# Fixing TensorE's order, turning k without it, and masking scores on two other engines in a gated-attention and SiLU kernel

## The chip, the cores and the metric

The kernel runs on one core of one Trainium2 chip. The metric is the time of one execution in device microseconds. Three runs of the kernel before took 563.61, 564.00 and 565.02 us, so the median is 564.0 us. The profiles come from one further execution each.

## The reference

Two blocks follow each other. The first is a recurrent gated attention over 4 batches, 8 heads, 768 tokens and 48 features for each head; the second is a feed-forward layer over the 3072 rows of its result.

```python
for t in range(S):                         # q, k, v, alpha: (4, 8, 768, 48)
    state = alpha[:, :, t, :, None] * state + einsum('bhd,bhe->bhde', k[:, :, t], v[:, :, t])
    y[:, :, t] = einsum('bhd,bhde->bhe', q[:, :, t], state)
x = y.transpose(0, 2, 1, 3).reshape(3072, 384)
h = x @ w_in                               # (384, 2048)
g = h * (1 / (1 + exp(-h)))
out = g @ w_out                            # (2048, 384)
```

The two weights arrive as 64-bit floats and are rounded to 32 bits on the chip.

## The kernel before

**Attention in chunks.** The sequence is cut into chunks of 128 tokens; with 4 batches that makes 24 chunks, numbered by `n`. A chunk is handled for all 8 heads at once, as 4 pairs of heads (`NP`). Each chunk passes through these stages:

- `products` (lines 674 to 715) brings alpha, k and q into a layout with features on partitions, scans alpha for its running product `u` (L699) and multiplies k by it (`kp`, L709, L713, L715). For the first 8 chunks (`n < NA`) TensorE turns the inputs (L694); later ones are loaded in quarters and turned by VectorE in blocks of 32x32 (L674).
- `quotient` divides: a second scan (L728) and a product with q (L733) give `qp`.
- `scores` multiplies kp by qp on TensorE (L757), cuts the result with the causal mask (`g`), turns kp into `kn` with tokens on partitions (TensorE L774, ScalarE copy L776) and scales the running state by the chunk's decay (L780). The mask is applied by ScalarE's copy and a GpSimd select (L763, L764) in chunks 0 to 3, and by VectorE's multiplication with a constant tile `mask` (L768) from chunk 4 on. From chunk 8 on only the halves of the scores that are needed are computed, so `blank` (L741) writes zeros into the PSUM banks beforehand.
- `values` forms y from g, v, the state and qp on TensorE (L800), and ScalarE copies it into `xt` (L805).
- `states` adds kn times v (L815) to the running state (VectorE L821).

The attention's PSUM tiles rotate through 3 banks (`ps_a`).

**Feed-forward pieces.** The dense work is cut into small pieces that are run between the attention stages. For the first two groups of 4 chunks the first layer is done plainly (`enter_plain`, L858, SiLU L861). From the third group on it is done with a fast matrix scheme that needs fewer products and more additions (`enter`: matmuls L882, ScalarE copies L888, VectorE additions L896, SiLU L893; `sums_x`, L562 to L567). The second layer is done in 7 products for each 2 chunks in the same manner (`leave`: matmuls L980, differences L985, copies L1010 and L1015, sums L1025 to L1036, stores L992 to L996). The chosen weights are rounded on the way in (`weights`: ScalarE L609, VectorE L623 to L625), and an audit reads the inputs once more and reduces them on VectorE (L653, L655, L663).

**The order of the work.** The program is written as 25 steps of 4 slots. In step `n`, slots are given to stages of chunk `n` (lag 0) and of chunk `n-1` (lag 1), and `fill` runs dense pieces after each slot until a running target is met (`marks`). A scheduler then reorders instructions on each engine, apart from the ones that `keep_in_program_order` holds in their stated order. All DMAs are issued by SP's queue: the loads of the next chunk's alpha, k and q (L465, 12 DMAs a chunk from chunk 8 on), of v (L482, L484), of the weights (L498), and the stores (L996).

The slots from chunk 8 on are:

```python
stages = [[(scores, 1)], [(products, 0)], [(values, 1), (states, 1)], [(quotient, 0), (blank, 0)]]
```

Of the kernel before, what the change touches and what calls it, by code (L numbers as in the profile page):

```python
# [355 lines left out]
def quotients(  # L356
# [20 lines left out]
    pe, dve, act, gps = nc.tensor, nc.vector, nc.scalar, nc.gpsimd  # L377
    B, H, S, D = q.shape
    C = 128
# [28 lines left out]
    rpool = pool("rpool")  # L408
    upool = pool("upool")
# [107 lines left out]
    def turns(x, n):  # L517

        return x[(n + 1) % 2 if n < NA else 0]
# [10 lines left out]
    mask = consts.tile([128, 2, C], F32, name="mask")  # L530
    gps.memset(mask, 1.0)
    for odd in range(2):
        for e in range(2):
            m = mask[CH * e : CH * e + CH, odd, :]
            gps.affine_select(m, m, pattern=[[1, C]], compare_op=ALU.is_ge, fill=0.0,
                              base=-CH * (e ^ odd), channel_multiplier=-1)
# [57 lines left out]
    def weights(which):  # L594

        pieces = [
            (w_in[:, t, c : c + 512], moe_w_in[t * 128 : t * 128 + 128, c : c + 512])  # L600
            for t, c in pieces_in
        ] if which == 0 else [
            (w_out[:, f, :], moe_w_out[f * 128 : f * 128 + 128, :]) for f in range(NFT)]
        def rounding(bits):
            n = bits.shape[1]
            up = upp.tile([128, 512], I32, name="up")[:, 0:n]

            tc.keep_in_program_order(
                act.activation(up, bits.bitcast(U32)[:, :, 0], AF.Copy, scale=2.0**-29))  # L609
            return up  # L610

        ahead = []
        for i, (dst, src) in enumerate(pieces):
            if not wide:
                act.dma_start(dst, src)
                yield
                continue
            assert which == 0 or conv_done[0] == n_conv[0]
            bits = coming.pop(0)
            up = ahead.pop() if ahead else rounding(bits)  # L620
            hi, w = bits[:, :, 1], dst.bitcast(I32)
            tc.keep_in_program_order(
                dve.tensor_scalar(w, hi, 3, 0x3FFFFFFF, ALU.logical_shift_left, ALU.bitwise_and))  # L623
            dve.scalar_tensor_tensor(w, hi, -(1 << 30), w, ALU.bitwise_and, ALU.bitwise_or)
            dve.tensor_tensor(w, w, up, ALU.add)  # L625
            if i + 1 < len(pieces):
                ahead.append(rounding(coming[0]))
            fetch()
            yield
# [46 lines left out]
    def products(n):  # L676
# [26 lines left out]
        kp = c["kp"] = turns(kps, n)  # L703
# [14 lines left out]
    def quotient(n, sg=None, q=None):  # L718
# [8 lines left out]
        p = turns(qps, n)  # L727
# [7 lines left out]
    def blank(n):  # L735

        if n < NA:
            return
        ps = ctxs[n]["blank"] = [ps_attn() for _ in range(2)]
        for t in ps:  # L740
            act.activation(t.rearrange("p j c -> p (j c)"), ident[:, 0:1].to_broadcast([128, 4 * C]),  # L741
                           AF.Copy, scale=0.0)

    def scores(n):
        c = ctxs[n]
        ci, b = c["ci"], c["b"]
        ps = c.pop("blank") if n >= NA else [ps_attn() for _ in range(2)]
# [11 lines left out]
        g = c["g"] = work.tile([128, 2, NP, C], F32, name="g")  # L759
        for u in range(2):  # L760
            if n < GB:

                act.copy(g[:, u], ps[u])  # L763
                gps.affine_select(g[:, u], g[:, u], pattern=[[0, NP], [1, C]], compare_op=ALU.is_ge,  # L764
                                  fill=0.0, base=0, channel_multiplier=-1)
                continue
            m = mask[:, :, None, :] if n >= NA else mask[:, 0:1, None, :]
            dve.tensor_tensor(g[:, u].rearrange("p (o j) c -> p o j c", o=2),  # L768
                              ps[u].rearrange("p (o j) c -> p o j c", o=2),
                              m.to_broadcast([128, 2, NP // 2, C]), ALU.mult)  # L770
        if ci < NCH - 1:
# [13 lines left out]
    def values(n):  # L785

        c = ctxs[n]
        ci, b, g, qp = c["ci"], c["b"], c["g"], c["qp"]
# [3 lines left out]
        todo = [(3 * j + i, vn[:, j, at : at + 32], g[:, u, j, :])  # L792
                for j in range(NP) for i, at, u in ((0, 0, 0), (1, 32, 0), (2, 80, 1))]
        todo += [(3 * j + 1, vn[:, j, 48:80], g[:, 1, j, :]) for j in range(NP)]
# [11 lines left out]
    def states(n):  # L806
        c = ctxs.pop(n)
        ci, b, vn = c["ci"], c["b"], c["v"]
        if ci < NCH - 1:

            ps = ps_attn()
            for j in range(NP):
                for i in range(4):
                    r = slice(32 * i, 32 * i + 32)
                    pe.matmul(ps[r, j, 0:D], lhsT=c["kn"][:, j, r], rhs=vn[:, 2 * j + i // 2, 0:D],  # L815
                              start=True, stop=True)
# [286 lines left out]
    marks = [2 * SLOTS + 2] + [(GB * i + 2 * GB) * SLOTS + 2 for i in range(len(phases))]  # L1103

    def settle():
# [4 lines left out]
        quads = pool("quads")  # L1110
        late["quads"] = {name: quads.tile([128, 32 + 4 * NP * D], F32, name=f"{name}t") for name in "akq"}
# [4 lines left out]
    def fill(step, slot):  # L1116

        at = step * SLOTS + slot
        if at < marks[0]:
            if step >= 1:  # L1120
# [12 lines left out]
    for step in range(STEPS):  # L1133
# [6 lines left out]
        elif step >= NA:  # L1140
            stages = [[(scores, 1)], [(products, 0)], [(values, 1), (states, 1)], [(quotient, 0), (blank, 0)]]
        for slot, group in enumerate(stages):
            for stage, lag in group:
# [8 lines left out]
                if stage is quotient and n + 1 < NT:  # L1152
                    load(n + 1)
                if stage is states and n + NV < NT:
                    load_v(n + NV)
            fill(step, slot)
# [23 lines left out]
    pe.matmul(ps, lhsT=good, rhs=mask[:, 0, C - 1 : C], start=True, stop=True)  # L1180
# [63 lines left out]
```

## Time and profile before

| | kernel before |
|---|---|
| median of 3 runs | 564.0 us |
| the profiled execution's own time | 563.47 us |
| its span, first to last instruction | 561.6 us |
| mean granted TensorE clock | 0.994 |
| TensorE (PE) busy | 543.9 us |
| VectorE (DVE) busy | 453.0 us |
| ScalarE (ACT) busy | 205.3 us |
| GpSimd (POOL) busy | 15.1 us |
| DMA | 63.81 MB, mean 114 GB/s |

A busy time counts an engine's instructions, with their ends modelled on TensorE, so a busy engine need not be working at its peak pace. In the profile every fp32 matmul other than a transpose shows as two records, so a product of 8 matmuls has 16. Lines such as L774 are lines of the kernel. In a timeline the columns are the start, the time that the row covers, engine, line, operation, operands and the count of records merged in the row; in brackets stands how long the engine was idle before it, and which engine released it.

### The profile page before, as it was taken

How to read it: one execution, taken by the hardware profiler on the slowest of the kernel's cores; microseconds unless marked ns; L12 is line 12 of the kernel's file. 1: busy time of each engine (PE TensorE's matmuls, PEld its weight loads, DVE VectorE, ACT ScalarE, POOL GpSimd, SP SyncE). 2: the span in 40 equal slices, each digit the busy share in tenths (PEclk: the TensorE clock that was granted, in tenths of full speed). 3: DMA queues.
4: the chain of work that ended last, by engine and by line, in shares of the span. 5: the costliest groups of instructions: out<-in, count | busy, mean ns of one | idle time of the engine just before them, and what ended most of it. 6: DMA issues, size and time to landing. Idle time of an engine off the chain costs nothing.

```text
span 561.6 us, 12420 instructions
## 1 busy us (share of the span) xinstructions
PE 543.9 (97%) x5074; PEld 492.6 (88%) x5074; DVE 453.0 (81%) x829; ACT 205.3 (37%) x406; POOL 15.1 (3%) x36
## 2 busy tenths in 40 slices
PE   5899999999999999999999999999999999999996
PEld 3688887998999999899989999999998999899995
DVE  5797899966999799986998897899895875857731
ACT  2566543213233342443433443434443342332100
POOL 4211000100000000000000000000000000000000
PEclk9899999999999999999999999999999999999998
DMA  9989971143443333333425544435522123334200
GB/s 206 230 241 223 234 183 34 43 126 100 100 107 89 73 97 87 101 87 85 131 70 160 142 108 134 130 81 153 136 69 81 53 85 118 99 94 125 71 30 26
DMA packets 94417, 63.81 MB, mean 114 GB/s; under 512 B 55312, under 2 KB 86032, under 8 KB 94352
## 3 DMA queue, kind: packets, MB, share of 16 engines
q1 hardware_dynamic: 94352, 62.94, 43.3%
q8 instruction: 41, 0.67, 0.5%
q14 instruction: 24, 0.20, 0.1%
HBM read 58.20 MB, written 4.72 MB: 112 GB/s over the span
## 4 chain that ended last, share of the span: by engine, by line
PE 75%; DVE 14%; DMA 5%; SPq 2%; issue 2%; ACT 1%; POOL 0%; DVEq 0%; ACTq 0%
PE ps_o L980 33%; PE ps_m L882 18%; PE ps_m L858 11%; PE ps_a L800 6%; DMA bits<-in_moe_w_out_dram 3%; PE ps_a L757 3%; DVE seen L663 2%; PE ps_a L774 1%; DVE g L896 1%; DMA bits<-in_moe_w_in_dram 1%; DVE u L699 1%; PE ps_a L815 1%; DVE w_out L625 1%; DVE p L728 1%; SPq L456 1%
## 5 line engine op out<-in xcount | busy, mean ns | idle before, releaser
L980 PE MATMUL ps_o<-w_out,g 128*128 128x192 f32 x768 | 133.6, 328 | 1.1 <-DVE o L994 1.1
L980 PEld LDWEIGHTS ps_o<-w_out,g 128*128 128x128 f32 x768 | 125.5, 190 | 3.9 <-DVE o L994 1.5
L980 PE MATMUL ps_o<-wt,g 128*128 128x192 f32 x576 | 100.0, 327 | 0.0
L980 PEld LDWEIGHTS ps_o<-wt,g 128*128 128x128 f32 x576 | 95.1, 190 | 1.5
L858 PE MATMUL ps_m<-xt,w_in 128*128 128x256 f32 x384 | 88.5, 382 | 1.0 <-ACT xt L805 1.0
L858 PEld LDWEIGHTS ps_m<-xt,w_in 128*128 128x128 f32 x384 | 71.0, 190 | 11.0 <-ACT xt L805 1.4
L882 PE MATMUL ps_m<-xc,w_in 128*128 128x256 f32 x288 | 70.1, 379 | 0.0
L882 PEld LDWEIGHTS ps_m<-xc,w_in 128*128 128x128 f32 x288 | 54.0, 190 | 6.4 <-DVE g L896 0.2
L663 DVE TENSOR_REDUCE seen<-bits 128x1 f32<-128x384 int32 (+2 forms) x65 | 42.4, 689 | 16.8 <-DMA bits<-in_moe_w_out_dram 16.5
L893 ACT ACTIVATE g<-g 128x1024 f32<-128x1024 f32 x32 | 33.1, 1055 | 57.5 <-DVE g L896 57.5
L985 DVE TENSOR_TENSOR g<-g 128x512 f32<-128x512 f32 x72 | 48.5, 686 | 5.6 <-PE ps_o L980 5.6
L882 PE MATMUL ps_m<-xc,wx 128*128 128x256 f32 x192 | 50.1, 383 | 0.0
L888 ACT COPY g<-ps_m 128x512 f32<-128x512 f32 x64 | 36.8, 587 | 36.1 <-PE ps_m L882 36.0
L780 ACT ACTIVATE st<-st,least 128x96 f32<-128x96 f32 x80 | 24.1, 364 | 58.4 <-DVE least L702 58.4
L882 PEld LDWEIGHTS ps_m<-xc,wx 128*128 128x128 f32 x192 | 35.0, 190 | 4.2 <-issue 0.4
L896 DVE TENSOR_TENSOR g<-ps_m,g 128x512 f32<-128x512 f32 x56 | 37.4, 683 | 0.8 <-PE ps_m L882 0.5
L699 DVE TENSOR_TENSOR_SCAN u<-al,one 128x516 f32<-128x516 f32 x24 | 29.1, 1212 | 10.4 <-ACT al L696 10.3
L728 DVE TENSOR_TENSOR_SCAN p<-al,inv 128x516 f32<-128x516 f32 x24 | 29.4, 1226 | 5.2 <-PE ps_a L800 4.9
L861 ACT ACTIVATE g<-ps_m 128x512 f32<-128x512 f32 x32 | 19.0, 595 | 39.2 <-PE ps_m L858 39.0
L800 PE MATMUL ps_a<-g,vn 128*32 128x128 f32 x768 | 28.0, 282 | 3.9 <-POOL g L764 3.9
L800 PEld LDWEIGHTS ps_a<-g,vn 128*32 128x32 f32 x768 | 20.3, 112 | 11.2 <-issue 5.5
L768 DVE TENSOR_TENSOR g<-ps_a,mask 128x512 f32<-128x512 f32 x40 | 25.7, 685 | 4.0 <-PE ps_a L757 3.7
(125 smaller groups left out, 620.7 us busy)
## 6 DMA issues: line engine op xcount, KB each, us to landing
bits<-in_moe_w_in_dram SPq DMA_DIRECT2D x24, 512.0 KB, 4.7
bits<-in_moe_w_out_dram SPq DMA_DIRECT2D x32, 384.0 KB, 3.4
at<-in_alpha_dram SPq DMA_DIRECT2D x64, 96.0 KB, 2.4
kt<-in_k_dram SPq DMA_DIRECT2D x64, 96.0 KB, 2.6
qt<-in_q_dram SPq DMA_DIRECT2D x64, 96.0 KB, 2.5
bits<-in_alpha_dram SPq DMA_DIRECT2D x9, 512.0 KB, 3.8
out_dram<-o SPq DMA_DIRECT2D x48, 96.0 KB, 1.9
an<-in_alpha_dram SPq DMA_DIRECT2D x8, 192.0 KB, 5.1
```

What stands on the lines that cost most here:

```text
L663: dve.tensor_reduce(seen[kind][which][:, i : i + 1], x, axis=AX, op=op, apply_absolute_value=True))
L699: dve.tensor_tensor_scan(u[:, end - 1 :: -1], sg[:, end:0:-1], one[:, end:0:-1], 0.0, ALU.mult, ALU.add)
L728: dve.tensor_tensor_scan(p[:, 0:end], sg[:, 0:end], iv[:, 0:end], 0.0, ALU.mult, ALU.add)
L768: dve.tensor_tensor(g[:, u].rearrange("p (o j) c -> p o j c", o=2), ps[u].rearrange("p (o j) c -> p o j c", o=2), m.to_broadcast([128, 2, ...
L800: pe.matmul(py[32 * at : 32 * at + 32, t, :], lhsT=w, rhs=x, start=(i < 4), stop=(i >= len(todo) - 4), skip_group_check=True)
L858: pe.matmul(ps[:, e, :], lhsT=w_in[:, t, (f + e) * 128 : (f + e + 1) * 128], rhs=xt[:, t, :], start=(t == 0), stop=(t == NKT - 1))
L882: pe.matmul(ps[:, e], lhsT=block_w(w)[:, 2 * pair + e], rhs=block_x(grp, x), start=(first and e == 0), stop=(e == 1), skip_group_check=True)
L888: act.copy(to, ps)
L893: act.activation(x, x, AF.Silu)
L896: dve.tensor_tensor(to, a, b, op)
L980: pe.matmul(ps, lhsT=x, rhs=w[:, i], start=(first and i == 0), stop=(i == HF - 1), skip_group_check=True)
L985: dve.tensor_tensor(cells(grp, h, pair, *to), cells(grp, h, pair, *x), cells(grp, h, pair, *y), ALU.subtract)
```

## The change

The change does five things.

- **TensorE in stated order.** `pe` becomes a small class whose `matmul` and `transpose` hold every instruction in its stated order. (In the changed program all TensorE instructions therefore carry the two lines of this class.)
- **Slots dealt anew.** From chunk 8 on: slot 0 `land` and `scores` of the chunk before, slot 1 `products`, slot 2 `quotient`, slot 3 `values` and `states` of the chunk before and `flip`. `p` gets a second buffer. The targets of `fill` move by one slot.
- **k turned by VectorE and by way of DRAM.** For chunks 8 to 19 `flip` turns kp in 32x32 blocks on VectorE, SP writes the result to a DRAM tile, and `land` reads it back with four DMAs in the order in which `states` needs it. Chunks 0 to 7 are turned by TensorE as before.
- **Masks by ScalarE and GpSimd.** VectorE's multiplication, the tile `mask` and `blank` go. Chunks 4 to 7 take the way of chunks 0 to 3. From chunk 8 on ScalarE copies only the halves that hold scores (two copies of 128x256 and four of 64x128), GpSimd selects in four pieces of 64x256, and the quarters that stay zero are cleared once.
- **Rounding moved.** The generator of the first weight stops once more: its ScalarE rounding is stated in slot 0 of step 1, its VectorE part a slot later.

```diff
-    pe, dve, act, gps = nc.tensor, nc.vector, nc.scalar, nc.gpsimd
+    dve, act, gps = nc.vector, nc.scalar, nc.gpsimd
+    class pe:
+        @staticmethod
+        def matmul(*args, **kw):
+            tc.keep_in_program_order(nc.tensor.matmul(*args, **kw))
+        @staticmethod
+        def transpose(*args):
+            tc.keep_in_program_order(nc.tensor.transpose(*args))
...
+    dram = pool("dram", 2, bass.MemoryType.DRAM)
...
+    decayed = fix.tile([128, 2 * NP * C], F32, name="g")
+    low, high = slice(0, CH), slice(CH, C)
+    earlier, later = [(low, 0), (high, 1)], [(low, 1), (high, 0)]
...
             up = ahead.pop() if ahead else rounding(bits)
+            if which == i == 0:
+                yield
...
-        p = turns(qps, n)
+        p = turns(qps if n < NA else [qps[0], late["p"]], n)
...
-    def blank(n):
...
+    def flip(n):
+        c = ctxs[n]
+        if n < NA or c["ci"] == NCH - 1:
+            return
+        t = late["turn"].tile([128, NP, C], F32, name="turn").rearrange("p c (j d) -> p c j d", j=NP)
+        dve.transpose(t, c["kp"].rearrange("p j (c i) -> p c j i", i=32))
+        c["flip"] = dram.tile([128, NP * C], F32, name="flips")
+        nc.sync.dma_start(c["flip"], t.rearrange("p c j d -> p (c j d)"))
+
+    def land(n):
+        c = ctxs[n]
+        if "flip" in c:
+            c["kn"] = work.tile([128, NP, C], F32, name="kn")
+            x = c.pop("flip").rearrange("(r d) (i x) -> i d r x", r=4, i=4)
+            for i in range(4):
+                nc.sync.dma_start(c["kn"][32 * i : 32 * i + 32], x[i])
...
-            m = mask[:, :, None, :] if n >= NA else mask[:, 0:1, None, :]
-            dve.tensor_tensor(g[:, u].rearrange("p (o j) c -> p o j c", o=2),
-                              ps[u].rearrange("p (o j) c -> p o j c", o=2),
-                              m.to_broadcast([128, 2, NP // 2, C]), ALU.mult)
-        if ci < NCH - 1:
+        for u in range(2 if n < NA else 0):
+            act.copy(g[:, u], ps[u])
+            gps.affine_select(g[:, u], g[:, u], pattern=[[0, NP], [1, C]], compare_op=ALU.is_ge,
+                              fill=0.0, base=0, channel_multiplier=-1)
+        if n >= NA:
+            ps = [x.rearrange("p (o j) c -> p o j c", o=2) for x in ps]
+            for u in range(2):
+                act.copy(swapped[:, :, u, :, CH:], ps[u][:, :, :, CH:])
+            for r, o in earlier:
+                for u in range(2):
+                    act.copy(swapped[r, o, u, :, 0:CH], ps[u][r, o, :, 0:CH])
+            for at, half in ((CH, later), (0, earlier)):
+                for r, o in half:
+                    x = swapped[r, o].rearrange("p u j c -> p (u j) c")[:, :, at : at + CH]
+                    gps.affine_select(x, x, pattern=[[0, NP], [1, CH]],
+                                      compare_op=ALU.is_ge, fill=0.0, base=0, channel_multiplier=-1)
+        if n < NA and ci < NCH - 1:
             ps_k = ps_attn()
             for j in range(NP):
                 pe.transpose(ps_k[:, j, :], c["kp"][:, j, :], ident)
...
-    marks = [2 * SLOTS + 2] + [(GB * i + 2 * GB) * SLOTS + 2 for i in range(len(phases))]
+    marks = [2 * SLOTS + 2] + [(GB * i + 2 * GB) * SLOTS + 3 for i in range(len(phases))]
...
-            if step >= 1:
+            if at == SLOTS:
+                next(conv[0])
+            elif step >= 1:
                 convert(0, (at - SLOTS) * 3 // (marks[0] - SLOTS) + 1)
...
-            stages = [[(scores, 1)], [(products, 0)], [(values, 1), (states, 1)], [(quotient, 0), (blank, 0)]]
+            stages = [[(land, 1), (scores, 1)], [(products, 0)], [(quotient, 0)],
+                      [(values, 1), (states, 1), (flip, 0)]]
...
+            if step * SLOTS + slot == (NA + 1) * SLOTS - 1:
+                x = decayed.rearrange("p (o i c) -> p o i c", o=2, c=C)
+                for r, o in later:
+                    gps.memset(x[r, o, :, 0:CH], 0.0)
```

## The prediction

> **What bounds the kernel now.** I read the page first (busy shares, then the chain of work that ended last), then the timeline of TensorE from 0 to 562 us, then the groups by form, the waits, and the order of instructions on each engine in both programs.
>
> ```profile
> PE 543.9 (97%) x5074; PEld 492.6 (88%) x5074; DVE 453.0 (81%) x829; ACT 205.3 (37%) x406; POOL 15.1 (3%) x36
> ...
> PE 75%; DVE 14%; DMA 5%; SPq 2%; issue 2%; ACT 1%; POOL 0%; DVEq 0%; ACTq 0%
> ```
>
> TensorE is busy for 97% of the span and makes up 75% of the chain. Because matmul ends are modelled, I checked the starts. In the timeline, 16 records of L980 take 2.60 us and 12 records of L882 or L858 take 2.59 us wherever they follow each other. From 25 us on, nearly every start comes at that pace. The stretch 25.18 to 128.69 us (103.5) is filled by its records at these paces (97 us) and some thirty switches of shape at 0.1 to 0.2 us. So from 25 us on, **a microsecond of TensorE work is a microsecond of the span**, and VectorE's 81% matters only where it makes TensorE wait. After 25 us the waits are few:
>
> ```profile
> 232.24 1.13 PE L882 MATMUL ps_m<-xt,w_in 128*128 128x256 f32 x4 [0.40 <-DVE g L896]
> ...
> 294.85 1.13 PE L882 MATMUL ps_m<-xt,w_in 128*128 128x256 f32 x4 [0.34 <-ACT g L888]
> ...
> 483.69 2.87 PE L980 MATMUL ps_o<-w_out,g 128*128 128x192 f32 x16 [1.07 <-DVE o L994]
> ```
>
> Measured by starts these three cost 0.7, 0.5 and 1.2 us, about 2.5 us with the smallest ones.
>
> **What the Trainium skill says.** "TensorE: Matmul & The Clock Gate", Part 4, puts a transpose at about 275 ns in a kernel. The trace's records agree (L774 median 273 ns), but they overlap: four take 0.4 to 0.5 us. "VectorE: DVE Perf Modes", The three transpose paths, says that VectorE transposes only inside 32x32 blocks; so the change needs DRAM to move the blocks. L674 shows its price, 1.11 us for 128x512. "DMA: Bandwidth & Descriptors", Anatomy of one DMA, gives about 2.0 us fixed for one transfer; the page agrees (1.9 us for an output store, 2.6 for a k load). "SBUF — State Buffer", Who interferes with whom, says a VectorE instruction with two SBUF inputs contends with a GpSimd one that reads SBUF. The trace has a sign of it: the two selects L764 took 1.94 us at 14.94 us beside VectorE's weight rounding and 1.23 us at 21.17 us with VectorE idle.
>
> **The change part by part.**
>
> *k turned without TensorE.* Of 20 chunks that turn k at L774, 12 (chunks 8 to 19) stop. The same program shows a step with and without it:
>
> ```profile
> 243.29 0.90 PE L757 MATMUL ps_a<-p,kp 48*64 48x128 f32 x32
> 244.12 0.66 PE L774 MATMUL ps_a<-ident,kp 128*128 128x128 f32 x4
> 244.62 1.03 PE L882 MATMUL ps_m<-xc,wx 128*128 128x256 f32 x4
> 245.48 1.03 PE L882 MATMUL ps_m<-xc,w_in 128*128 128x256 f32 x4
> ...
> 413.62 0.90 PE L757 MATMUL ps_a<-p,kp 48*64 48x128 f32 x32
> 414.45 1.13 PE L882 MATMUL ps_m<-xc,wx 128*128 128x256 f32 x4
> 415.42 1.03 PE L882 MATMUL ps_m<-xc,w_in 128*128 128x256 f32 x4
> ```
>
> From the scores to the second L882 row it is 2.19 us with the turn (243.29 to 245.48) and 1.80 without (413.62 to 415.42). So 12 x 0.40 = **4.8 us** leave the bound, nearly certain (4.5 to 5.2).
>
> What it adds lies elsewhere. VectorE: 12 transposes at 1.11 = 13.3 us. SP: 12 x 5 issues at about 0.44 (its k loads) = 26 us over some 250; 6.3 MB, and the DMA engines are at 0.3 to 0.45 of capacity there. The trip is one store (2 us), then four loads (4 x 0.44 + 2.6): some 6.5 us. It starts late in step n, its loads stand in slot 0 of step n+1, and `states` reads in slot 3. A step takes 21 us, so over 10 us are left. What waits behind it on SP: in the new order half of the next chunk's alpha loads and all its k and q loads stand behind the store, and behind v's loads, which wait for `states`. From `states` on, SP needs 3 v and 1 or 2 alpha issues and a landing, about 4.5 us; VectorE has 4.7 to 4.8 us of other work before it transposes alpha. This is tight: 0 to 1 us of VectorE wait a step, and scores stand more than a slot later. I take 0 on TensorE. `turn` has one buffer, so the next k also waits for the store; some 10 us of VectorE work lie between.
>
> *Masks.* VectorE loses 40 multiplications (25.7 us busy) and, late, its wait for scores. ScalarE loses 32 blanks (L741, 0.60) and 12 copies of k (0.58), gains 2 copies 128x256 and 4 of 64x128 a late chunk. By its copies of 512, 384 and 192 columns (587, 475, 315 ns) these are 0.37 and 0.26, so 1.78 a step: just what leaves (2 x 0.60 + 0.58). Chunks 4 to 7 add 8 x 0.59. GpSimd gains 8 selects at 0.87 and 64 half-size ones (estimate 0.3 to 0.55 each, from L764's 0.63 to 1.08 for twice the columns): 19 to 35 us on an engine that does nothing there. If each half-size one holds VectorE up by 0 to 0.2 us (weight rounding beside L764 ran 0.2 to 0.4 long), that is 0 to 13 us of VectorE. Its balance is -25.7 + 13.3 + (0 to 13): 12 us less to nothing. Mask latency is scores to select, about 4 us, and y now stands five pieces (13 us) behind the scores. Cost on the path: nothing while that cover stands.
>
> *Slots and order.* The quotient moves from slot 3 to 2, y and states from 2 to 3, p gets two buffers. So qp is ready a slot before its scores, and VectorE's wait for y (L728, 4.9 us) goes. The price: scores now follow y by a single piece, 2.6 us, on three PSUM buffers, and the second scores bank is y's. It is free once ScalarE has copied y (L805), which in every second step stands behind four SiLUs (L893) that wait for VectorE. Today's example: y ends at 363.7, the SiLUs at 364.8, so the copy could end at 365.3, 1.6 us after y; the scores would want it 3.1 us after. 1.5 us of room. I take +1.0 us in all, between 0 and 16 (1 us in every late step). For the old waits that vanish I take -1.0 (0 to -2.5).
>
> *Rounding.* At the start the static order on ScalarE puts one weight rounding before the first scores' copies where there were two, and the second waits for its DMA:
>
> ```profile
> 11.39 0.69 ACT L609 ACTIVATE up<-bits 128x512 int32<-128x512 uint32 x1 [1.92 <-DMA bits<-in_moe_w_in_dram]
> ...
> 13.73 0.67 ACT L609 ACTIVATE up<-bits 128x512 int32<-128x512 uint32 x1 [1.65 <-DMA bits<-in_moe_w_in_dram]
> ...
> 14.30 1.05 ACT L763 COPY g<-ps_a 128x512 f32<-128x512 f32 x2
> ...
> 14.94 1.94 POOL L764 TENSOR_SCALAR_AFFINE_SELECT g<-g 128x512 f32<-128x512 f32 x2 [7.91 <-ACT g L763]
> ...
> 15.89 0.64 PE L800 MATMUL ps_a<-g,vn 128*32 128x128 f32 x4 [3.62 <-POOL g L764]
> ```
>
> The copies can start near 12.1, 2.2 us sooner. Not all gets through: the third L858 piece met its weights just in time (32.23 to 32.54 us), and VectorE's w_out chain ends at 101.5 us where TensorE waits 0.23; that chain loses one mask pair, 1.3 us. I take -1.3 (0 to -2.2).
>
> *Sum.* -4.8 - 1.3 - 1.0 + 1.0 = -6.1 us. The profiled run took 563.5 us (span 561.6 and 1.9 around it), 0.5 under the median of three, 564.0. So 557.4 by the profiled run, 557.9 by the median; I say **557.5 us**.
>
> **Rivals.** (1) *The bound holds and the sum comes through*, 553 to 562 us, 0.64. For it: the saturated timeline, and a part that is counted, not inferred. (2) *Only the turn is saved and small new waits eat it*: VectorE is busy 33 to 39 of each 40 us between 200 and 440, so a late load, a select on the shared port or a late L896 each hold TensorE a little; no gain at the start, +4 us: 563 us, 0.13. (3) *Slower: the bank of y.* If SiLUs and so the y copy come later than the 1.5 us of room, TensorE stops at the scores with all its dense work behind it. From a mean of 0.44 us on each of 16 late steps it uses up the gain of 7.1 us that stands without it, from 0.6 the kernel is measurably slower; at 1 us a step it gives 557.5 - 1 + 16 = 572 us. For it: ScalarE waits 57.5 us for L896 before L893, up to 6.7 at a time. Against it: most of that is ScalarE early, not TensorE late. 0.23. That k still comes from TensorE in part can be excluded: the new order has no such transposes after chunk 7.
>
> **How the numbers follow.** 0.3% (1.7 us) is about what a measurement of this kernel can tell from no change: 562.3 and 565.7 are the edges. Case 1 is faster throughout; of case 2, 0.03 is faster and 0.10 the same; case 3 is slower. So 0.67, 0.10, 0.23. The range, 553 to 568, leaves some 0.04 below (all waits gone and the start's full gain) and 0.15 above (rival 3 from 0.7 us a step). Case 1's own range is 553 to 562.
>
> **What would show it.** Right: no L774 rows after chunk 7; L757 followed within 0.85 us by a dense row; first L800 near 13.7 us; late steps some 0.4 us shorter; no TensorE wait above 0.5 us at scores or at `states`. Wrong: TensorE waits before L757 released by ScalarE's y copy (rival 3), before `states` by the loads of k (trip too slow), or VectorE above 92% in the late stretches with TensorE waiting for L896 (rival 2).

## The result, and the profile after

The changed kernel takes 580.05 us (median of 4 runs, 578.9 to 581.0), the kernel before in the same rounds 563.81. The ratio is 1.0286, with a 95% interval of 1.0258 to 1.0315: **slower by 16.1 us** (0.0286 x 563.81). The forecast was 557.5 us, range 553 to 568. The profiled execution has a span of 579.2 us.

This is the page of the changed kernel: the busy shares, the slices of TensorE and of its granted clock, and the chain that ended last. Every TensorE instruction now has line L384 (matmul) or L388 (transpose), so it is read by its tiles. The *trip* below is the new way of k: VectorE's flip (L757), its store to DRAM (L759), the four loads back (L767).

```profile
PE 544.3 (94%) x5026; PEld 491.0 (85%) x5026; DVE 446.1 (77%) x801; ACT 207.7 (36%) x466; POOL 50.1 (9%) x106
...
PE   5899998999998999999999799599999999999996
...
PEclk9999999999999999999999799989999999999999
...
PE 57%; DVE 18%; DMA 14%; SPq 5%; issue 2%; ACT 2%; POOL 0%; DVEq 0%; ACTq 0%
```

TensorE has 48 instructions less, as foreseen, yet the same busy time. Its share of the chain fell from 75% to 57%; DMA rose from 5% to 14% and SP's queue from 2% to 5%. VectorE is *less* busy than before. There are two holes in TensorE's row, each with a lower clock in the same slice or the next. The timeline of TensorE shows them:

```profile
321.40 0.52 PE L384 MATMUL ps_a<-vn,kn 128*32 128x48 f32 x32
326.11 5.23 PE L384 MATMUL ps_o<-w_out,g 128*128 128x192 f32 x16 [4.18 <-DVE o L1028]
331.27 0.90 PE L384 MATMUL ps_a<-p,kp 48*64 48x128 f32 x32
332.10 1.13 PE L384 MATMUL ps_m<-xc,w_in 128*128 128x256 f32 x4
...
369.95 0.52 PE L384 MATMUL ps_a<-vn,kn 128*32 128x48 f32 x32
376.60 5.49 PE L384 MATMUL ps_o<-w_out,g 128*128 128x192 f32 x16 [6.12 <-DVE o L1028]
```

After the state products, TensorE waits for VectorE to empty the bank of an output (L1028), 4.2 and 6.1 us long. In both cases an audit of 1.2 to 1.3 us (L677) stands right ahead of that instruction in VectorE's order. The product that follows takes 5.23 and 5.49 us where 16 matmuls of this kind take 2.76 to 2.87 elsewhere. The windows view (busy time of each engine, then granted clock) has the reason:

```profile
core 0: us, PE busy (x) PEld busy (x) DVE busy (x) ACT busy (x) POOL busy (x), PEclk, DMA share, GB/s
...
326.00:331.30 5.30, 5.19 (x20) 4.97 (x20) 1.97 (x5) 0.00 (x0) 0.00 (x0) 0.53 0.80 207
...
376.60:382.00 5.40, 5.40 (x16) 4.97 (x16) 3.50 (x9) 0.00 (x0) 0.00 (x0) 0.50 0.90 229
```

The clock is at half after each stop. So the two stops cost 4.2 + 2.5 and 6.1 + 2.7, together 15.5 us, nearly the whole difference. The rest roughly cancels. The start gained what was foreseen (first y product at 13.85 us instead of 15.89; first dense piece at 23.44 instead of 25.18), and undisturbed late steps are 21.4 and 20.5 us from y to y instead of 21.8 and 20.9. Smaller waits eat that gain.

**Why VectorE was late.** These are VectorE's waits for DMAs from 128 to 455 us, after (in all, times, longest), together 20.2 us, and then the only row of before in that window for a turn of alpha, k or q or for the audit:

```profile
DVE al L688 <- DMA at<-in_alpha_dram: 11.1, 6, 4.6
...
DVE al L688 <- DMA kt<-in_k_dram: 3.9, 3, 2.9
DVE seen L677 <- DMA bits<-in_alpha_dram: 2.6, 1, 2.6
DVE seen L677 <- DMA bits<-in_moe_w_in_dram: 2.6, 2, 2.4
```

```profile
DVE al L674 <- DMA at<-in_alpha_dram: 0.5, 1, 0.5
```

Now SP's queue in one step of the changed kernel, with its neighbour VectorE (start, duration). First SP, from one store of the flipped k to the next:

```profile
299.94 0.32 SPq L759 DMA_DIRECT2D flips<-turn  x1
300.31 0.92 SPq L478 DMA_DIRECT2D at<-in_alpha_dram  x2
301.64 0.35 SPq L667 DMA_DIRECT2D bits<-in_alpha_dram  x1
302.08 0.96 SPq L495 DMA_DIRECT2D vn<-in_v_dram  x1
303.14 1.27 SPq L497 DMA_DIRECT2D vn<-in_v_dram  x2
304.45 1.07 SPq L478 DMA_DIRECT2D at<-in_alpha_dram  x2
305.57 1.85 SPq L478 DMA_DIRECT2D kt<-in_k_dram  x4
307.46 1.85 SPq L478 DMA_DIRECT2D qt<-in_q_dram  x4
309.36 2.93 SPq L767 DMA_DIRECT2D kn<-flips  x4
...
322.30 0.33 SPq L759 DMA_DIRECT2D flips<-turn  x1
```

Then VectorE in the same step:

```profile
306.40 1.22 DVE L677 TENSOR_REDUCE seen<-bits 128x1 f32<-128x1024 f32 x1 [2.65 <-DMA bits<-in_alpha_dram]
308.13 1.11 DVE L688 STREAM_TRANSPOSE al<-at 128x512 f32<-128x512 f32 x1 [0.51 <-DMA kt<-in_k_dram]
...
321.56 0.71 DVE L757 STREAM_TRANSPOSE turn<-kp 128x512 f32<-128x512 f32 x1
...
324.58 1.21 DVE L677 TENSOR_REDUCE seen<-bits 128x1 f32<-128x1024 f32 x1
325.71 0.35 DVE L1028 TENSOR_TENSOR o<-ps_o,u 128x192 f32<-128x192 f32 x1
```

The rows show a **loop of two in-order queues**. The store waits on SP for VectorE's flip, the last thing VectorE does for a chunk; SP issued nothing from 294.93 to 299.94 us. Over the window such waits are 35.6 us (SP's waits at the output's stores are longer, 75.4 us, but before they were 63.5):

```profile
SPq L759 <- DVE turn L757: 35.6, 8, 6.8
```

The Trainium skill says why it is SP that stands ("DMA: Bandwidth & Descriptors", Anatomy of one DMA): the DMA engines don't wait on semaphores, the issuing queue does, ahead of the issue. The trace agrees: the idle 5.0 us are SP's. The next chunk's alpha, k and q, the audit and v stand behind the store in SP's order. VectorE turns alpha when it has landed, and 13.4 us after that comes to the next flip. Store to store is 22.36 us here, while TensorE's own step is 20.5 (21.4 every second time). With every engine in order, VectorE is late for whatever it meets next, and in the two stops that is L1028. That the store alone closes this loop is not shown: one of the experiments (e7_loads_pool) opens it with the store still in SP's queue.

How far ahead the loads run can be counted: from the end of the last issue of alpha (L465, L478) to VectorE's turn of it (L674, L688), over chunks 8 to 23. Before, the median is 13.2 us, and over 12 in the last nine chunks. After, the median is 2.6 us; in 12 of 16 chunks it is between 1.9 and 3.1, about the time that an alpha load takes to land (2.4 us). The lead was gone in those chunks. A long lead isn't needed, though: the fastest kernel below (c2_masks_old_slots) has a median of 4.2.

### The profile page after: what moved, and what is told of

Same layout as the page of the kernel before. It is cut to its first block, busy times and chain, and to the rows that moved or that the text cites. A ratio compares the mean times of both kernels' runs of the same rounds, so it can differ in the third digit from the quotient of the medians.

```text
span 579.2 us, 12563 instructions
## 1 busy us (share of the span) xinstructions
PE 544.3 (94%) x5026; PEld 491.0 (85%) x5026; DVE 446.1 (77%) x801; ACT 207.7 (36%) x466; POOL 50.1 (9%) x106
## 4 chain that ended last, share of the span: by engine, by line
PE 57%; DVE 18%; DMA 14%; SPq 5%; issue 2%; ACT 2%; POOL 0%; DVEq 0%; ACTq 0%
PE ps_o L384 25%; PE ps_m L384 23%; PE ps_a L384 8%; DMA bits<-in_moe_w_out_dram 7%; DVE seen L677 3%; DVE g L930 3%; SPq L478 3%; DVE turn L688 2%; DMA bits<-in_moe_w_in_dram 2%; PE ps_a L388 1%; DMA kn<-flips 1%; DMA qn<-in_q_dram 1%; DVE u L713 1%; SPq L767 1%; DVE g L1019 1%
## 5 line engine op out<-in xcount | busy, mean ns | idle before, releaser
L384 PE MATMUL ps_o<-w_out,g 128*128 128x192 f32 x768 | 139.6, 337 | 13.0 <-DVE o L1028 11.6
L384 PEld LDWEIGHTS ps_o<-w_out,g 128*128 128x128 f32 x768 | 130.1, 196 | 17.2 <-DVE o L1028 13.1
L384 PE MATMUL ps_m<-xt,w_in 128*128 128x256 f32 x480 | 113.7, 383 | 3.1 <-ACT xt L838 2.8
L384 PEld LDWEIGHTS ps_m<-xt,w_in 128*128 128x128 f32 x480 | 89.0, 190 | 16.6 <-ACT xt L838 3.8
L384 PE MATMUL ps_o<-wt,g 128*128 128x192 f32 x576 | 99.7, 326 | 0.0
L384 PEld LDWEIGHTS ps_o<-wt,g 128*128 128x128 f32 x576 | 95.1, 190 | 1.6 <-issue 0.2
L384 PE MATMUL ps_m<-xc,w_in 128*128 128x256 f32 x288 | 70.7, 382 | 0.4 <-ACT part L922 0.4
L677 DVE TENSOR_REDUCE seen<-bits 128x1 f32<-128x384 int32 (+2 forms) x65 | 42.5, 689 | 25.4 <-DMA bits<-in_moe_w_out_dram 18.8
L384 PEld LDWEIGHTS ps_m<-xc,w_in 128*128 128x128 f32 x288 | 53.7, 190 | 7.4 <-ACT part L922 0.7
L802 POOL TENSOR_SCALAR_AFFINE_SELECT g<-g 64x256 f32<-64x256 f32 x64 | 29.8, 466 | 291.2 <-ACT g L795 288.1
L384 PE MATMUL ps_m<-xc,wx 128*128 128x256 f32 x192 | 50.0, 383 | 1.0 <-ACT g L922 1.0
L922 ACT COPY g<-ps_m 128x512 f32<-128x512 f32 x64 | 36.6, 586 | 35.8 <-PE ps_m L384 35.6
L930 DVE TENSOR_TENSOR g<-ps_m,g 128x512 f32<-128x512 f32 x56 | 37.2, 682 | 4.8 <-PE ps_m L384 4.5
L384 PEld LDWEIGHTS ps_m<-xc,wx 128*128 128x128 f32 x192 | 35.2, 190 | 5.2 <-ACT g L922 1.3
L688 DVE STREAM_TRANSPOSE al<-at 128x512 f32<-128x512 f32 x16 | 17.8, 1115 | 16.6 <-DMA at<-in_alpha_dram 12.6
L922 ACT COPY part<-ps_m 128x512 f32<-128x512 f32 x32 | 18.7, 585 | 26.9 <-PE ps_m L384 21.3
```

The costliest lines, as they stand in the source:

```text
L384: tc.keep_in_program_order(nc.tensor.matmul(*args, **kw))
L677: dve.tensor_reduce(seen[kind][which][:, i : i + 1], x, axis=AX, op=op, apply_absolute_value=True))
L688: dve.transpose(to.rearrange("p g (b j) -> p g j b", j=4), x[:, :, :, 0:32])
L802: gps.affine_select(x, x, pattern=[[0, NP], [1, CH]], compare_op=ALU.is_ge, fill=0.0, base=0, channel_multiplier=-1)
L922: act.copy(to, ps)
L930: dve.tensor_tensor(to, a, b, op)
```

## The experiments

Two theories stood at first. Q: the trip's DMAs in SP's queue starve VectorE. O: the stated order and the new slots make the stops by themselves. A third, M, put it on the masks. In the expectations, "checks" are the kernel's audit (L677).

### One part taken away or done alone

**k back on TensorE** (e1_k_on_pe), so no flip, store or loads:

```diff
-        if n < NA or c["ci"] == NCH - 1:
-            return
+        return
...
-        if n < NA and ci < NCH - 1:
+        if ci < NCH - 1:
             ps_k = ps_attn()
```

> The changed kernel, but k is turned by TensorE again in all chunks (four transposes and ScalarE's copy), so VectorE's turn of k, its store to DRAM and its four loads are gone; order, slots, masks and rounding stay as changed. Theory Q (the trip's DMAs stand in SP's queue ahead of the next chunk's loads, VectorE starves, falls behind and stops TensorE at the first product of an output): the two stops of 4.2 and 6.1 us at L384 (ps_o) are gone with their slow products, some 15.6 us, a few of the small stops as well, and 4.8 us of turns come back: about 567 us, 562 to 570. Theory O (the stated order and the new slots make the stops by themselves): the stops stay, 580 + 4.8 = 585, 582 to 588. Theory M (the masks on ScalarE and GpSimd delay VectorE): also 582 to 588.

Measured: 569.5 us, ratio to before 1.0093 (1.0066 to 1.0121), 10.5 us below the changed kernel though 4.8 us of turns (the forecast's figure) are back. Both long stops are gone. Theory Q holds for these; 5.3 us above before stay.

**The trip on GpSimd's queue** (e2_trip_pool):

```diff
-        nc.sync.dma_start(c["flip"], t.rearrange("p c j d -> p (c j d)"))
+        gps.dma_start(c["flip"], t.rearrange("p c j d -> p (c j d)"))
...
-                nc.sync.dma_start(c["kn"][32 * i : 32 * i + 32], x[i])
+                gps.dma_start(c["kn"][32 * i : 32 * i + 32], x[i])
```

> The changed kernel, but the trip's store and its four loads of k are issued from GpSimd's queue instead of SP's; VectorE still turns k and the same bytes move. Theory Q: SP is free for the next loads, VectorE's waits for alpha, k and the audited data go from 12.6 us to about before's 1, the two long stops go: 564 us, 556 to 568. Theory O or M: nothing of it matters, 578 to 583. If it is the volume of the trip on the DMA engines and not its place in the queue, the waits stay too: 578 to 583. A new wait may come: the masks (L802) stand behind the loads in GpSimd's queue, then y waits for them.

Measured: 568.3 us, ratio 1.0061 (1.0041 to 1.0081). The bytes are the same, so the volume was not the cause: 11.8 us hung on the queue, and on the order in which SP's other DMAs then stand. The time is just above theory Q's range. VectorE's waits for alpha, k, q and the audit did not go to 1 us but from 20.2 to 10.5, and in e1_k_on_pe to 7.8: what counts is not their sum but what stands behind each.

**TensorE's order left free** (e4_pe_free):

```diff
-            tc.keep_in_program_order(nc.tensor.matmul(*args, **kw))
+            nc.tensor.matmul(*args, **kw)
```

(and likewise for the transposes)

> The changed kernel, but TensorE's order is left to the scheduler instead of stated. Theory O: it can go around the late eviction bank, the two stops of 4.2 and 6.1 us go: 564 us, 560 to 568. Theory Q: VectorE is late whatever TensorE does, stops of this size stay at the first product of an output or move: 576 to 584; the scheduler puts the state products next to the following scores, so loads of k may show up less.

Measured: 572.9 us, 1.0147 (1.0121 to 1.0173). It lies between the two. The longest wait at L1028 in the profile is 1.3 us, so the free order goes around the late bank, but it moves the state products and steps become uneven (27 and 15 us). So the two long stops needed a late VectorE *and* a TensorE that may not do other work.

**The kernel before with the order stated** (b1_order_only):

```diff
-    pe, dve, act, gps = nc.tensor, nc.vector, nc.scalar, nc.gpsimd
+    dve, act, gps = nc.vector, nc.scalar, nc.gpsimd
+
+    class pe:
+        @staticmethod
+        def matmul(*args, **kw):
+            tc.keep_in_program_order(nc.tensor.matmul(*args, **kw))
+
+        @staticmethod
+        def transpose(*args):
+            tc.keep_in_program_order(nc.tensor.transpose(*args))
```

> The kernel before, with TensorE's order stated and nothing else changed. Theory O with the stated order as its cause: 570 us or more. Theory Q or M: no change, 563.8 plus or minus 1.7.

Measured: 566.8 us, 1.0042 (1.0026 to 1.0057). The stated order costs 2.4 us, more than the 1.7 that theories Q and M allowed for, less than the 6 of O. In its profile y is 2.0 us later than before at 110.68 us and 2.4 at 447.60. TensorE waits for a w_in piece (1.57 us at 50 us) and for ScalarE's y copies: 0.60, 0.60 and 1.47 us at 24, 58 and 91 us. In b2_rounding below, with the order free, the waits for the same copies are 0.26, 0.27 and 0.43. The wait for w_in shows in some profiles with the stated order and not in others.

**Only the rounding moved** (b2_rounding):

```diff
             up = ahead.pop() if ahead else rounding(bits)
+            if which == i == 0:
+                yield
...
-            if step >= 1:
+            if at == SLOTS:
+                next(conv[0])
+            elif step >= 1:
```

> The kernel before with nothing but the rounding moved (the first weight rounding on ScalarE stated a slot later). My forecast's term: -1.3 us (0 to -2.2), 562.5. If the start is bound by the arrival of the weights further on, the gain at the first y product (about 2 us) is gone by 50 us and the time is that of before, 563 to 565.

Measured: 562.1 us, 0.9965 (0.9954 to 0.9976): 2.0 us faster.

**Masks and rounding in the old slots** (c2_masks_old_slots), order free, k on TensorE:

```diff
-            stages = [[(land, 1), (scores, 1)], [(products, 0)], [(quotient, 0)],
-                      [(values, 1), (states, 1), (flip, 0)]]
+            stages = [[(scores, 1)], [(products, 0)], [(values, 1), (states, 1)], [(quotient, 0)]]
```

(with `marks` at + 2 again, the next load after the quotient, and the edits of the first and third experiment)

> Masks on ScalarE and GpSimd and the rounding moved, but with the slots of before, TensorE's order left to the scheduler, and k turned by TensorE in all chunks: the kernel before with the masks changed, in short. Theory M (the masks cost): 566 or more. If VectorE's relief is worth what I took (nothing on the path), 562.5 plus or minus 1.5.

Measured: **560.6 us, 0.9944 (0.9924 to 0.9964), the version that beats both kernels.** The masks, with the second buffer of `p` that is in this kernel too, are worth 1.2 to 1.5 us on top of the rounding (562.1 to 560.6; 0.9965 to 0.9944); the two intervals just overlap. Theory M falls. TensorE has no wait above 0.2 us after 128 us in this profile.

**The new slots alone** (e5_k_on_pe_free): the edits of the first and third experiment on the changed kernel.

> The changed kernel with k turned by TensorE in all chunks and TensorE's order left to the scheduler: what is left of the change is the new slots, the masks and the rounding. If the stated order costs as in the kernel before (2.5 us), 567. If the new slots are what costs the rest, it stays 3 us or more above the kernel with masks in the old slots.

Measured: 567.6 us, 1.006 (1.0042 to 1.0078), so 7.0 us above the last kernel, from which it differs in the slots only (with `marks` and the place of the next load, that go with them). The stated order adds 2.0 (569.5 against 567.6), as it did in the kernel before.

### Which DMA, which buffer, which engine

**Only the four loads of k moved to GpSimd's queue** (e7_loads_pool), the store left on SP's: the second half of the e2_trip_pool diff.

> The changed kernel, with only the four loads of k on GpSimd's queue; the store of the flipped k stays on SP's. If the store is what holds SP up (it waited 35.6 us for VectorE's flip), little comes back: 576 to 580. If it is the four loads, that wait for the store's landing and take 4 issues, most of the 11.8 us comes back: 568 to 571.

Measured: 567.7 us, 1.0075 (1.0047 to 1.0103). Everything that e2_trip_pool gave comes back with the loads alone. In this kernel the static order of SP's queue is another one too. SP's queue in its profile, over one such stretch:

```profile
279.89 1.86 SPq L478 DMA_DIRECT2D at<-in_alpha_dram  x4
288.18 0.35 SPq L667 DMA_DIRECT2D bits<-in_alpha_dram  x1
288.57 0.91 SPq L478 DMA_DIRECT2D kt<-in_k_dram  x2
293.21 0.34 SPq L759 DMA_DIRECT2D flips<-turn  x1
294.32 0.35 SPq L667 DMA_DIRECT2D bits<-in_alpha_dram  x1
294.71 0.90 SPq L478 DMA_DIRECT2D kt<-in_k_dram  x2
298.24 0.36 SPq L1030 DMA_DIRECT2D out_dram<-o  x1
298.64 2.73 SPq L478 DMA_DIRECT2D qt<-in_q_dram  x4
301.47 0.38 SPq L478 DMA_DIRECT2D at<-in_alpha_dram  x1
```

And GpSimd's, with the wait ahead of the loads:

```profile
300.13 2.17 POOL L767 DMA_DIRECT2D kn<-flips  x4 [15.59 <-PE ps_a L384]
```

Here the loads were held for 15.6 us by TensorE: `kn` has one buffer, and the state products of the chunk before read it until 300 us. On SP's queue it is not this wait that held the next chunk back: in the changed kernel's trace SP shows no wait ahead of these four loads (L767). They stand last, behind a burst of the next chunk's loads (309.36 us above), and by then `kn` is free. Of the trip's DMAs it is the store at which SP waits. What the move changed is the order: in the step of the changed kernel shown above, the next chunk's alpha, k and q all stand behind the store, while here all four loads of alpha and two of k were issued ahead of it, and the median lead of alpha is 5.1 us instead of 2.6. It also took four issues a step, some 1.9 us, off SP. How much each of these is worth was not separated.

**The trip in the old slots, GpSimd's queue** (c1_trip_old_slots), otherwise as c2_masks_old_slots, which the expectation calls the kernel just described:

```diff
+            stages = [[(scores, 1)], [(products, 0), (flip, 0)], [(values, 1), (states, 1), (land, 0)],
+                      [(quotient, 0)]]
```

> As the kernel just described, but k of chunks 8 to 19 is turned by VectorE and by way of DRAM: the flip stated right after the products of the chunk, its loads of k after the states of the chunk before, both on GpSimd's queue, so that the trip has three slots. If the trip costs nothing where it has time and a queue of its own: 4.8 us under the kernel with masks in the old slots, about 558. If the trip itself (VectorE's time, DMA volume) costs: within 1.5 us of that kernel or above it.

Measured: 569.5 us, 1.0089 (1.0068 to 1.011), 9 above the same slots without the trip. VectorE's timeline names a part:

```profile
147.69 1.10 DVE L688 STREAM_TRANSPOSE turn<-qt 128x512 f32<-128x512 f32 x1 [1.11 <-DMA flips<-turn]
...
148.96 0.68 DVE L747 TENSOR_TENSOR p<-turn,p 128x512 f32<-128x512 f32 x1
```

and TensorE's what follows from it:

```profile
149.78 0.90 PE L384 MATMUL ps_a<-p,kp 48*64 48x128 f32 x32 [1.47 <-DVE p L747]
```

`turn` has one buffer, so the turn of q waits for the store of the flipped k, and the scores wait for q.

**A buffer of its own for the flip** (c3_trip_own_buffer), the chunk's k tile, already read:

```diff
-        t = late["turn"].tile([128, NP, C], F32, name="turn").rearrange("p c (j d) -> p c j d", j=NP)
+        t = late["quads"]["k"][:, 32 : 32 + NP * C].rearrange("p (c j d) -> p c j d", c=NP, j=NP)
```

> The trip of k in the old slots on GpSimd's queue, as tried before, but the flipped k is put into the chunk's own k tile, which VectorE has already read, and no longer into the single buffer turn, where the turn of q had to wait for the store. If that buffer was what cost (5.2 us of VectorE waits on the store, and q late at the scores), the 4.8 us of turns show at last: 556 to 558 against 560.6 of the kernel with masks in the old slots. If it is VectorE's time or the transfers themselves, it stays near 569.

Measured: 564.6 us, 1.000 (0.9992 to 1.0009). The buffer was worth 4.9 us, on balance: the k tile is also what the next loads of k fill, and SP waits there for the store to have read it:

```profile
SPq L478 <- DMA flips<-kt: 11.9, 7, 5.2
```

It is neither of the two outcomes: still 4 us above the kernel with k on TensorE.

**The same on SP's queue** (c4_trip_own_buffer_sp): `nc.sync` for `gps` in both DMAs.

> The same, but store and loads of the trip on SP's queue. Theory Q (SP's queue is the cost, in any slots): 8 us or more above the same kernel with GpSimd's queue, 565 to 572. If the queue only hurt because the trip stood in the last slot, right ahead of the next loads: within 2 us of it.

Measured: 582.1 us, 1.0336 (1.0298 to 1.0374), worse than expected, and in slots where the trip has most time. SP's queue is the cost in these slots too, but not all 17.5 us need be its waits: the scheduler, left free, also laid the steps out unevenly (up to 29 and down to 15 us), as in e4_pe_free.

**No flip on VectorE** (c5_no_flip): k is stored as it stands, without the turn.

```diff
-        dve.transpose(t, c["kp"].rearrange("p j (c i) -> p c j i", i=32))
...
-        gps.dma_start(c["flip"], t.rearrange("p c j d -> p (c j d)"))
+        gps.dma_start(c["flip"], c["kp"].rearrange("p j c -> p (j c)"))
```

> The trip of k in the old slots on GpSimd's queue without VectorE's flip: the unflipped k is stored straight from its own tile and loaded as before, so the state products read wrong numbers; store and loads, bytes and queue stay. If VectorE's 12 flips (0.71 us each, 8.5 us) are what keeps the trip 4 us above the kernel with k on TensorE in place of 4.8 below: 555.5 to 558. If the transfers or GpSimd's queue cost it (later alpha loads, masks behind the k loads): it stays at 562 to 565.

Measured: 559.5 us, 0.9921 (0.99 to 0.9942): 5.1 us less than with the flips. That is the price of 12 flips (8.5 us of VectorE) together with their place in the k tile: with the flip, SP's wait of 11.9 us for that tile went as well, and VectorE's waits for alpha, k and the audit fell from 18.0 to 10.9 us. How much of the 5.1 us is VectorE's time alone is not shown. The kernel is 1.1 us under the one with k on TensorE and not 4.8. Of the 3.7 left, 1.6 are three waits for VectorE's L928 between 216 and 272 us; the rest was not traced.

### The tail of the new slots

From the last attention product to the end, the new slots need 118.3 us (e5_k_on_pe_free), the kernel before 114.7, so 3.6 us more.

**Another phase of the audit** (e9_audit_phase): `turns = 1` for `turns = 0` ahead of the tail's loop.

> The kernel with new slots, k on TensorE and the order left free, with one edit in the tail: the reads of the checks (L677) are dealt one and two output pieces apart in the other phase, so that another VectorE instruction stands behind each. The new slots' tail is 3.4 us longer than before's from 452 us on, with waits for SiLU (L926, 1.4) and L1027 (1.45). If the place of the checks in VectorE's queue makes these, they change: 2 to 3.5 us less, 564 to 566. If the tail is longer for another reason: within 1 us of 567.6.

Measured: 567.5 us, 1.0051 (1.0033 to 1.0069): no difference. It shifted only every second audit, by one piece.

**Two pieces ahead of the last audits** (e11_audit_two):

```diff
     turns = 0
+    for _ in range(2):
+        go_on()
     while next(audits, 0) is None:
```

> The kernel with new slots, k on TensorE and the order left free, with two output pieces stated ahead of the last reads of the checks. Counting pieces by the due times shows that the new slots have done 135 of 176 at the end of the loop where the old ones had done 137, so every check in the tail stood two pieces earlier; the earlier test moved only every second one, by one. If that is the tail's 3.6 us, it goes: 563.5 to 565, with no wait at L926 and less at L1027. If not, 567.5.

Measured: 563.9 us, 0.9994 (0.9983 to 1.0005): 3.7 us back. VectorE's timeline of the new slots without the edit (e5_k_on_pe_free):

```profile
520.91 0.35 DVE L1027 TENSOR_TENSOR o<-ps_o,u 128x192 f32<-128x192 f32 x1
521.81 1.01 DVE L677 TENSOR_REDUCE seen<-bits 128x1 f32<-128x384 int32 x2 [0.56 <-DMA bits<-in_moe_w_out_dram]
522.74 1.28 DVE L929 TENSOR_TENSOR g<-ps_m,g 128x512 f32<-128x512 f32 x2
```

and with it:

```profile
519.40 0.35 DVE L1027 TENSOR_TENSOR o<-ps_o,u 128x192 f32<-128x192 f32 x1
519.67 0.68 DVE L929 TENSOR_TENSOR g<-ps_m,g 128x512 f32<-128x512 f32 x1
521.29 1.01 DVE L677 TENSOR_REDUCE seen<-bits 128x1 f32<-128x384 int32 x2 [0.94 <-DMA bits<-in_moe_w_out_dram]
```

The audit, which waits for its DMA, stood ahead of the last additions, so their SiLU was late and TensorE waited 1.4 us for it (L926). The new `marks` had moved two dense pieces out of the loop, and so every audit two pieces forward.

### Repairs together

**All three repairs** (e14_sum): loads of k on GpSimd's queue, free order, two pieces ahead of the last audits.

> The changed kernel with the three repairs together: the loads of k on GpSimd's queue, TensorE's order left free, two pieces ahead of the last checks. If the costs add as measured (12.4, 2.0, 3.6): 580 - 18 = 562, between 560.5 and 564. If the free order goes wrong with the trip, as it did with SP's queue: 566 or more.

Measured: 568.7 us, 1.007 (1.0046 to 1.0094). The costs don't add with the free order.

**Two of them, order stated** (e15_pool_and_two): without the free order.

> The changed kernel, order stated as changed, with two repairs: the loads of k on GpSimd's queue and two pieces ahead of the last checks. If these two costs are separate: 567.7 - 3.6 = 564, 563 to 565.5. If they act on each other as the three repairs together did with the free order (568.7 instead of 562): 567 or more.

Measured: 566.8 us, 1.005 (1.0033 to 1.0067). Only 0.9 of the 3.6 us came back by the medians, 1.6 by the profiled spans (565.6 to 564.0): the wait for SiLU in the tail is gone, a wait for L1028 of 0.45 is new. The costs act on each other, and why they do so was not settled.

## Why the prediction was wrong, step by step

By medians, undoing the parts in this order: rounding -2.0, masks -1.5, new slots +7.0, stated order +2.0, k by way of SP's queue +10.5. That is +16.0, and the measured difference is +16.1. In another order the parts differ (the free order alone gave 7.2 us back from the changed kernel).

- **k turned without TensorE, -4.8: right for a step, and not got.** Undisturbed late steps are 0.4 us shorter, as forecast. But the part as a whole measured +10.5, 15.3 us off.
- **SP's queue, "0 to 1 us of VectorE wait a step ... I take 0 on TensorE": this is the step that failed.** The DMAs behind the store were listed rightly. VectorE then waited 15.0 us for alpha and k, 1.0 a step over the window's late steps, the edge of what I gave, and 5.2 more for the audit. The error was to end there. A wait of VectorE was taken as lost on VectorE only, because scores stand more than a slot later; what stands behind it in VectorE's queue is also the eviction of an output bank, which TensorE needs at once after the states. The two stops with their slow clock are 15.5 us, and the part measured +10.5 with its gain of 4.8 in it. The distance to scores was not safe either: at 178.24 us TensorE waited 1.76 us there for q's product (L747), after VectorE had waited 3.07 us for alpha at 167.35. And I compared one step's slack (4.7 against 4.5) where a loop repeats: in the chunks with the short lead nothing let the loads catch up.
- **The trip itself, "over 10 us are left": right.** TensorE waited for `kn` once, 0.3 us. The store took 2.6 us to land (I took 2), a load of k 2.0; the Trainium skill's 2.0 us fixed for one transfer, which I took for it ("DMA: Bandwidth & Descriptors", Anatomy of one DMA), is given there for transfers issued by GpSimd, and was near enough on SP's queue. A trip that is in time can still stop others.
- **VectorE's flips, 13.3 us:** they took 0.70 each, 8.4 in all. I priced them by L674's 1.11 for the same 128x512, but the access pattern is another. I put their cost on the path at nothing; the run without them is 5.1 us faster in the old slots, a wait for the k tile included.
- **`turn` has one buffer, "some 10 us of VectorE work lie between":** no wait on it shows in the changed kernel; with an early flip, in the old slots, a buffer elsewhere gave 4.9 us back.
- **Masks, 0: nearly right**, -1.2 to -1.5. Prices held, as the groups by form show:

```profile
L802 POOL TENSOR_SCALAR_AFFINE_SELECT g<-g 64x256 f32<-64x256 f32 x64 | 29.8, 466 | 291.2 <-ACT g L795 288.1
L798 ACT COPY g<-ps_a 64x128 f32<-64x128 f32 x64 | 13.6, 263 | 0.4
L795 ACT COPY g<-ps_a 128x256 f32<-128x256 f32 x32 | 10.3, 372 | 10.7 <-PE ps_a L384 10.7
L757 DVE STREAM_TRANSPOSE turn<-kp 128x512 f32<-128x512 f32 x12 | 8.4, 703 | 0.2
```

- **Slots and order, +1.0 between 0 and 16: mis-sized**, 9.0 by the runs. What I had in view, the bank of y behind the SiLUs, cost nothing: no wait above 0.25 us ahead of scores is released by ScalarE's y copy, so rival 3 gave the right side by the wrong mechanism. The 9.0 are 3.7 of audits in the tail, 2.0 of the stated order, 2.4 of two waits of k's turn on a PSUM bank that only the kernels with k on TensorE in the new slots have (1.65 and 0.73 us in e1_k_on_pe), and 0.9 not traced. (Without these two waits the kernel with k on TensorE would have been 2.4 faster, and the trip on SP's queue by as much dearer.) I never costed the stated order: I looked at where instructions move, not at waits that a free order fills.
- **Old waits vanish, -1.0: not got.** The waits at 232 and 295 us went, but others of their kind came (0.69 at 227.51 and 0.99 at 246.78 us), and the one at L980 (483.69 before) stayed as 0.93 at L1028.
- **Rounding, -1.3 (0 to -2.2): right**, -2.0 by the runs. Here is the first y product of the changed kernel, which I had put near 13.7:

```profile
13.85 0.41 PE L384 MATMUL ps_a<-g,vn 128*32 128x128 f32 x4 [1.54 <-POOL g L790]
```

- **The signs that I named:** of the right forecast, "no TensorE wait above 0.5 us at scores" failed once, with the 1.76 us above. Of the wrong one, TensorE waits neither for the y copy nor for k beyond 0.3 us. In stretches of 40 us from 200 to 440, VectorE is above 92% only from 200 to 240 (38.5 of 40; before 38.7), where TensorE waits 0.69 us for L930 (L896 before); in the two stretches with the stops it is busy for 28.5 and 34.5 of 40. None of these pointed to the stops. The sign to look for was a load that VectorE waits for.

## What to carry to other kernels

When a DMA that waits for a late engine is put into a queue that also feeds that engine, follow the circle: the store, the loads behind it, their landing, the engine's work up to the next store. Here it was 22.4 us long against a step of 20.5 to 21.4, and the lead of the loads was gone in most chunks, whatever the busy shares said. Look at the order in which such a queue is issued, too: here it was enough to take four loads off it that showed no wait of their own; part of the next chunk's loads then stood ahead of the store. And price a wait of a helper engine by what stands behind it in that engine's own queue, down to the instruction that the bounding engine needs next.

## What was not expected of the hardware

Two stops of TensorE, 4.2 and 6.1 us, were each followed by 5.2 to 5.5 us at a granted clock of 0.53 and 0.50, so the price of the stop was 1.4 to 1.6 times its length. A stop of 1.94 us (e2_trip_pool) was not: the four matmuls after it took 1.13 us, as at any change of shape. These stops agree with the Trainium skill ("TensorE: Matmul & The Clock Gate", Part 1: half clock after an idle window of about 3.4 us and until a busy one has passed). Others don't fit a window without work: in c1_trip_old_slots two waits of 1.76 and 1.09 us, with 1.1 us of matmuls between them, left TensorE busy for 1.56 of the 3.6 us from 222.0 to 225.6, and from there to 229.0 the clock was 0.50. And at the start of e1_k_on_pe a stop of 1.71 us ahead of the first y product was followed by a clock of 0.51 from 15.7 to 22.6 us, while the changed kernel's 1.54 us at that place was not. So a shorter stop can cost clock as well, and its length alone doesn't tell. I had no stop of such length in the forecast, though the kernel before shows one: with the 3.62 us ahead of its first y product came a clock of 0.51 from 15.5 to 19.0 us.

VectorE's block transpose of 128x512 took 0.70 us for L757 and 1.12 for L688, which differ in their access patterns.
